# Releasing GpSimd's subtraction by a one-column VectorE copy, and reordering ScalarE's work, in a fused attention and two-layer kernel

## The chip, the cores and the metric

The kernel runs on one core of one Trainium2 chip. The metric is the device time of one execution in microseconds (us). Engines are named as in the profile: PE is TensorE (its weight loads are PEld), DVE is VectorE, ACT is ScalarE, POOL is GpSimd, SP is SyncE, which issues nearly all DMAs in one queue, in order.

## The reference, cut to what matters

Three stages follow one another on 2304 tokens (4 x 576) of 512 features:

```python
# chunked attention: 8 heads of 64, softmax inside chunks of 64 tokens
scores = scale * q_c @ k_c^T;  attn = softmax(scores);  x = attn @ v_c
# first network, w_in 512 x 2048, w_out 2048 x 512
h = x @ w_in;  x = (h - tanh(h)) @ w_out
# second network, same sizes
h = x @ w_in;  y = (h * tanh(softplus(h))) @ w_out
```

All of it is float32. The kernel reaches float32 accuracy by splitting each operand into a high and a low part (type fp32r) and adding three products, hi*hi, hi*lo and lo*hi (THREE, L338).

## The kernel before, in words

**Blocks and steps.** The tokens are cut into five blocks (BLOCKS, L38: 512, 256, 512, 512, 512). For each block the first network's 2048 hidden features are walked in NF = 16 tiles of 128. One (block, tile) pair is a step; there are NS = 80, in the list `steps` (L328), and the loop at L811 goes through them. In step s PE computes the hidden tile (`gemm1`, L340, 12 matmuls into one of two PSUM banks, `hidden(s)`) and, some steps later, multiplies it by w_out into four banks that gather the block's output (`gemm2`, L350, 12 matmuls). From step 36 on gemm2 lags by three steps (`lag`, L503): gemm2(s-3) is issued in step s. In step 38 no gemm2 is issued, because the lag grows there.

**The gap between them.** h - tanh(h) loses digits for small h, so a polynomial is used there. For step s:

- `gap_act` (L394), on ACT: Square of the bank into z, and Tanh into t. Between the two a list `between` is run, in the late steps `hi_part(s-2)`.
- `gap_mid` (L401), on DVE: the product g = z * bank, and the difference t = bank - t. Both read the PSUM bank.
- `gap_poly` (L407), on ACT: Relu of z into the mask m, and a second Square, which writes z in place. It therefore waits until DVE's product has read z.
- `gap_end` (L388), on DVE and one step later: g = (z + PK) * g (L390), and COPY_PREDICATED of t into g by the mask (L391).
- `hi_part` (L412), on ACT: the high part of g into go[:, 0]. `lo_part` (L428), on POOL from step 32 on: the low part, g minus the high part, into go[:, 1] (helper line L82). gemm2 reads both.

**Order inside a late step** (s > `late` = 36; the branch at L835). Each engine takes its instructions in the order in which the loop writes them: gemm1(s); DVE's gap_end(s-1); ACT's Square(s), hi_part(s-2), Tanh(s); POOL's lo_part(s-2), released by ACT's high part; DVE's gap_mid(s); the plan `inner`; `second(s)`, which issues gemm2; the plan `outer`; ACT's gap_poly(s); then the plans `cast` (ACT), `tail`, `w_again` (reloads of weights) and `job` (DVE and SP).

**Attention in between.** Tiles of 128 tokens of the next block are computed in four steps s to s+3 (L482 to L498). Step s: `a_scores` on PE (inner), then in the tail `a_first`, that is `a_max` on DVE and `a_exp` on ACT. Step s+1: `a_norm` on DVE. Step s+2: `a_turn`, transposes on PE, after gemm2, and `a_turned` on ACT, which copies them to SBUF as et (tail). Step s+3: `a_values` on PE, between gemm1 and gemm2, reads et; `a_part` writes the high part (ACT, L323) and the low part (DVE) of the block's x (tail).

**Units.** From step `first_job` = 35 on, the second network's weights are turned on the chip into sums and differences for a fast matrix product (seven products in place of eight) and stored in DRAM as win and wout. The table JOBS (L517) has a row for each of 16 units: its number, the step of its load (1 MB, `j_load`, SP), and the steps of its casts on ACT (j_turn L104, j_low L189, j_hi L210) and its work on DVE (join L113, sums and low parts L82). Five units are loaded at once when the pool "j" opens in step 35 (L816). Odd weights w of the first network are kept in DRAM as w1s and reloaded by `w_again` (L168, DMA at L175) when a slot of the ring of three is free.

**The end of the first network.** From step 69 (XFROM) x chunks are loaded into one tile `spare` (L422) and split (`x_sum`, `x_split`) in steps 73 to 78. In memory the pool "late" takes the place of the pool "j". After the loop come the last parts of the gap, gemm2 of the last steps, and `evacuate(NB-1)` with its stores of x1 (L377). The weights of the second network are loaded by `wf_load` (L594), cast by `wf_hi` (ACT) and `wf_lo` (DVE). `wf_lo` issues the next load (L611 to L617):

```python
elif part and j % 2:
    wf_load(p, j - 1, 1)
elif part and j + 3 < NJ:
    wf_load(p, j + 3, 1)
```

So the load of (0, 0, 1) is issued by wf_lo(0, 1, 1), behind the stores of evacuate in SP's queue. After that the loop at L931 runs `group1` (product1, L631) and `phase2` (slot2, L732) three times.

**Homes of the first weights.** At the start the first four token tiles are loaded whole into the slots of weights that come later: `home((0, NF - 3, NF - 1, NF - 2)[i])` (L234), that is w13, w15 and w14; those three weights are loaded after the first attention (L471). Slots lie in the pool in the order in which they were first taken, so w14's comes first in the pool "w", whose place the pool "f" (wf_load) takes over at the end.

Of the kernel before, what the change touches and what calls it, by code (L numbers as in the profile page):

```python
# [8 lines left out]
F32 = mybir.dt.float32  # L9
# [15 lines left out]
SQ_SCALE = PD ** 0.5  # L25
# [22 lines left out]
def attn_moe_moe(ctx, tc, qkv, w1, w2, out):  # L48
# [182 lines left out]
    def a_load(i, part=None):  # L231

        if 0 < i < first[1]:
            pool, tag = home((0, NF - 3, NF - 1, NF - 2)[i])  # L234
            t = pool.tile([P, 2 * DM], I64, tag=tag, name="qkv", bufs=1)[:].bitcast(F32)[:, :3 * DM]
            QK[i], V[i] = t[:, :2 * DM], t[:, 2 * DM:]
            nc.sync.dma_start(out=t, in_=qkv[i])
            return
        if part != 1:
            QK[i] = pools["a"].tile([P, 2 * DM], F32, tag="qk", name="qk", bufs=1)  # L240
            nc.sync.dma_start(out=QK[i], in_=qkv[i][:, :2 * DM])
        if part != 0:
            V[i] = pools["a"].tile([P, DM], F32, tag="v", name="v", bufs=2)
            nc.sync.dma_start(out=V[i], in_=qkv[i][:, 2 * DM:])
# [82 lines left out]

    steps = [(b, f if b != 3 else NF - 1 - f) for b in range(NB) for f in range(NF)]  # L328
# [65 lines left out]
    def gap_act(s, between=()):  # L394
        ph = hidden(s)
        z, t, m, g = ZT[s] = temp(s, "z"), temp(s, "t"), temp(s, "m", BF16), temp(s, "g")
        nc.scalar.activation(z, ph, AF.Square)  # L397
        run(*between)
        nc.scalar.activation(t, ph, AF.Tanh)  # L399
# [7 lines left out]
    def gap_poly(s):  # L407
        z, t, m, g = ZT[s]
        nc.scalar.activation(m, z, AF.Relu, bias=-C2)
        nc.scalar.activation(z, z, AF.Square, scale=SQ_SCALE, bias=SQ_BIAS)  # L410
# [9 lines left out]
    XG = {}  # L420

    def spare(k, n):  # L422

        if not XG:
            XG[0] = xp.tile([P, KD, 2 * TMAX], F32, tag="x1", name="spare")
        return XG[0][:, k, :n]
# [12 lines left out]
    for f in range(NF - 3):  # L439
        w_load(f)  # L440
# [18 lines left out]
    def run(*todo):  # L459
# [11 lines left out]
        (a_load, lead), (a_load, lead + 1, 1), (w_load, NF - 3), (w_load, NF - 2), (w_load, NF - 1),  # L471
# [4 lines left out]
    first_job = 2 * NF + 3  # L476
    inner, outer, tail, head, mid, post = {}, {}, {}, {}, {}, {}
# [4 lines left out]
    for b in range(1, NB):  # L482
        for q in range(BLOCKS[b] // P):
# [4 lines left out]
            at(tail, s, (a_first, i))  # L488
# [3 lines left out]
            at(outer if s + 2 > first_job + 1 else inner, s + 2, (a_turn, i))  # L492
            at(tail, s + 2, (a_turned, i))
            at(inner, s + 3, (a_values, i))
            at(tail, s + 3, (a_part, i, 0))
# [16 lines left out]
    def units(s, ahead):  # L512
# [7 lines left out]
        (9, 35, 41, 41, 44, 44, 45, 46, 47, 46, 47),  # L520
        (1, 35, 42, 43, 45, 45, 46),
        (10, 35, 43, 44, 46, 48, 48, 49, 50, 49, 51),
# [32 lines left out]
    def x_load(c):  # L555
        p, c = divmod(c, 4)
        t = pools["x"].tile([P, 4, TH // 2], F32, tag=("xa", "xb")[c % 2], name="xs")[:] if p else (
            spare(c, 2 * TH).rearrange("p (q n) -> p q n", q=4))
# [49 lines left out]
    def wf_lo(p, j, part):  # L608
        t = W2[p, j, part]
        sub(t[:, 1], WF.pop((p, j, part)), t[:, 0].bitcast(F32))  # L610
        if part == 0 and j + 2 < NJ:  # L611
            if p + j:
                wf_load(p, j + 2, 0)
        elif part and j % 2:
            wf_load(p, j - 1, 1)
        elif part and j + 3 < NJ:
            wf_load(p, j + 3, 1)  # L617
# [184 lines left out]
    late = first_job + 1  # L802
    XFROM = 4 * NF + 5

# [6 lines left out]
    for s in range(NS):  # L811

        if s == first_job:
            eo.close()
            pools["j"] = er.enter_context(tc.tile_pool(name="j", bufs=1, side="right"))
            for n, start, *_ in JOBS:  # L816
                if start == first_job:
                    j_load(n)
# [16 lines left out]
        if s > late:  # L835
            gap_act(s, [(hi_part, behind)] if behind >= late else [])
            if behind >= late:
                lo_part(behind)
            gap_mid(s)
            run(*inner.pop(s, []))  # L840
            second(s)
# [60 lines left out]
    assert not streamed and not job and not cast and not tail and not inner and not outer and ends + 6 < NS  # L902
# [23 lines left out]
    wf_load(0, 2, 0)  # L926
    evacuate(NB - 1)
# [56 lines left out]
```

## Time and profile before

| | us |
|---|---|
| median of 3 runs | 857.38 (856.44 to 857.4) |
| the profiled execution, its own time | 856.95 |
| its span in the trace | 855.2 |
| PE busy | 816.2 (95%) |
| PEld busy | 730.6 (85%) |
| DVE busy | 662.3 (77%) |
| ACT busy | 503.6 (59%) |
| POOL busy | 75.7 (9%) |

How to read it: the span is what the trace covers, and 1.75 us lie around it. The shares are means over stages that differ: the first network's steps end at about 500 us, and behind them the second network runs. In the rows a line has the start, the duration, the engine, the line of code, the operation, what is written and read, how many instructions were merged, and in brackets how long the engine stood idle before it and which instruction ended that. L82 and L85 are helpers (subtract, add); there the names of the tiles tell which work it is.

### The profile page before, as it was taken

How to read it: one execution, taken by the hardware profiler on the slowest of the kernel's cores; microseconds unless marked ns; L12 is line 12 of the kernel's file. 1: busy time of each engine (PE TensorE's matmuls, PEld its weight loads, DVE VectorE, ACT ScalarE, POOL GpSimd, SP SyncE). 2: the span in 40 equal slices, each digit the busy share in tenths (PEclk: the TensorE clock that was granted, in tenths of full speed). 3: DMA queues.
4: the chain of work that ended last, by engine and by line, in shares of the span. 5: the costliest groups of instructions: out<-in, count | busy, mean ns of one | idle time of the engine just before them, and what ended most of it. 6: DMA issues, size and time to landing. Idle time of an engine off the chain costs nothing.

```text
span 855.2 us, 13350 instructions
## 1 busy us (share of the span) xinstructions
PE 816.2 (95%) x5244; PEld 730.6 (85%) x5244; DVE 662.3 (77%) x916; ACT 503.6 (59%) x783; POOL 75.7 (9%) x64
## 2 busy tenths in 40 slices
PE   7899999999899979989999889999999999999997
PEld 6677778998677768768888679999999999999997
DVE  6999976865688897888887838878688787587653
ACT  3887966665665676575856535554455456345432
POOL 0001100001111222221221200000000000000000
PEclk9899999999999999999999999999999999999999
DMA  9975526626556686866585144398633788433873
GB/s 371 419 256 114 144 50 225 239 80 259 209 179 247 228 280 212 308 228 217 201 286 200 43 135 130 136 340 293 241 105 93 292 295 298 158 113 134 295 260 112
DMA packets 59071, 180.18 MB, mean 211 GB/s; under 512 B 4736, under 2 KB 32896, under 8 KB 46592
## 3 DMA queue, kind: packets, MB, share of 16 engines
q1 hardware_dynamic: 57568, 174.08, 57.3%
q0 software_dynamic: 1440, 5.24, 3.3%
q8 instruction: 41, 0.67, 0.3%
q14 instruction: 22, 0.18, 0.1%
HBM read 134.22 MB, written 39.85 MB: 204 GB/s over the span
## 4 chain that ended last, share of the span: by engine, by line
PE 57%; DVE 24%; DMA 7%; ACT 6%; issue 5%; SPq 1%; POOL 0%; DVEq 0%; ACTq 0%; POOLq 0%
PE banks L732 21%; PE banks L631 20%; PE banks L355 8%; PE banks L346 7%; DVE unit L82 3%; DVE g L390 3%; DVE g L404 3%; DMA w<-w1s 3%; DVE t L82 2%; DMA w<-wf 2%; DVE unit L113 2%; DVE wf L113 1%; DMA wout<-unit 1%; DVE g L391 1%; ACT unit L104 1%
## 5 line engine op out<-in xcount | busy, mean ns | idle before, releaser
L355 PE MATMUL banks<-go,w 128*128 128x512 f32 (+1 forms) x960 | 224.8, 384 | 7.0 <-POOL go L82 3.3
L346 PE MATMUL banks<-x,w 128*128 128x512 f32 (+1 forms) x960 | 218.7, 376 | 8.6 <-DMA w<-w1s 3.1
L355 PEld LDWEIGHTS banks<-go,w 128*128 128x128 f32 x960 | 172.4, 194 | 44.8 <-POOL go L82 4.7
L346 PEld LDWEIGHTS banks<-x,w 128*128 128x128 f32 x960 | 169.0, 191 | 44.5 <-DVE g L404 3.5
L631 PE MATMUL banks<-xo,w 128*128 128x384 f32 x1008 | 176.1, 334 | 3.0 <-ACT w L606 2.6
L732 PE MATMUL banks<-s,w 128*128 128x384 f32 x1008 | 178.6, 340 | 0.0
L631 PEld LDWEIGHTS banks<-xo,w 128*128 128x128 f32 x1008 | 174.7, 188 | 4.0 <-ACT w L606 2.9
L732 PEld LDWEIGHTS banks<-s,w 128*128 128x128 f32 x1008 | 178.1, 188 | 0.0
L82 DVE TENSOR_TENSOR s<-g,s 128x768 fp32r<-128x768 f32 x84 | 79.9, 957 | 44.8 <-ACT s L719 44.4
L719 ACT CAST s<-g 128x768 fp32r<-128x768 f32 x84 | 69.6, 835 | 62.4 <-PE banks L732 57.2
L82 POOL TENSOR_TENSOR go<-g,go 128x512 fp32r<-128x512 f32 x48 | 66.2, 1380 | 311.0 <-ACT go L418 290.9
L410 ACT ACTIVATE z<-z 128x512 f32<-128x512 f32 (+1 forms) x80 | 47.2, 589 | 63.9 <-DVE g L404 62.9
L404 DVE TENSOR_TENSOR g<-z,banks 128x512 f32<-128x512 f32 (+1 forms) x80 | 50.1, 626 | 41.1 <-ACT t L399 41.0
L82 DVE TENSOR_TENSOR w<-wf,w 128x1024 fp32r<-128x1024 f32 (+1 forms) x53 | 58.2, 1099 | 24.1 <-ACT w L606 23.6
L397 ACT ACTIVATE z<-banks 128x512 f32<-128x512 f32 (+1 forms) x80 | 43.9, 549 | 47.9 <-PE banks L346 47.9
L391 DVE COPY_PREDICATED g<-m,t 128x512 f32<-128x512 int16 (+1 forms) x80 | 67.8, 847 | 2.8
L606 ACT CAST w<-wf 128x768 fp32r<-128x768 f32 (+1 forms) x47 | 43.8, 934 | 39.2 <-DMA wf<-win 24.9
L390 DVE SCALAR_TENSOR_TENSOR g<-z,g 128x512 f32<-128x512 f32 (+1 forms) x80 | 58.2, 728 | 3.7 <-ACT z L410 3.7
L643 ACT ACTIVATE g<-g 128x768 f32<-128x768 f32 x36 | 30.5, 847 | 46.5 <-DVE g L85 46.5
L85 DVE TENSOR_TENSOR o<-o,banks 128x768 f32<-128x768 f32 x39 | 37.1, 951 | 19.5 <-PE banks L732 12.6
L82 DVE TENSOR_TENSOR t<-banks,t 128x512 f32<-128x512 f32 (+1 forms) x80 | 50.4, 630 | 0.0
L418 ACT CAST go<-g 128x512 fp32r<-128x512 f32 (+1 forms) x80 | 45.8, 573 | 7.6 <-DVE g L391 7.5
(70 smaller groups left out, 671.6 us busy)
## 6 DMA issues: line engine op xcount, KB each, us to landing
w<-wout SPq DMA_DIRECT2D x42, 1024.0 KB, 5.7
w<-w SPq DMA_DIRECT2D x16, 1024.0 KB, 19.7
unit<-w SPq DMA_DIRECT2D x16, 1024.0 KB, 6.9
w<-w1s SPq DMA_DIRECT2D x15, 1024.0 KB, 6.2
wf<-win SPq DMA_DIRECT2D x23, 512.0 KB, 3.6
wf<-win SPq DMA_DIRECT2D x24, 384.0 KB, 3.1
w1s<-w SPq DMA_DIRECT2D x8, 1024.0 KB, 7.6
qk<-qkv SPq DMA_DIRECT2D x15, 512.0 KB, 5.6
```

What stands on the lines that cost most here:

```text
L82: (eng or nc.vector).tensor_tensor(o, a, b, op=ALU.subtract)
L346: nc.tensor.matmul(ps, w[:, a, k * P:(k + 1) * P], x[:, c, k, :BLOCKS[b]], start=n == 0, stop=n == 3 * KD - 1)
L355: nc.tensor.matmul(banks[:, m, :t], w[:, a, DM + m * P:DM + (m + 1) * P], g[:, c, :t], start=s % NF == 0 and n == 0, stop=s % NF == NF - 1 ...
L390: nc.vector.scalar_tensor_tensor(g, z, PK, g, op0=ALU.add, op1=ALU.mult)
L391: nc.vector.copy_predicated(g, m.bitcast(I16), t)
L397: nc.scalar.activation(z, ph, AF.Square)
L404: nc.vector.tensor_tensor(g, z, ph, op=ALU.mult)
L410: nc.scalar.activation(z, z, AF.Square, scale=SQ_SCALE, bias=SQ_BIAS)
L418: nc.scalar.copy(o[:, 0, :BLOCKS[steps[s][0]]], GF[s])
L631: nc.tensor.matmul(ps, w[:, x, c % 4, k * P:(k + 1) * P], XO[p][:, a, y, k], start=m == 0 and n < 4, stop=m == 5, skip_group_check=n > 3)
L719: nc.scalar.copy(t[:, 0], src)
L732: nc.tensor.matmul(ps[:, m], w[:, x, k % 2 * 2 + e, m * P:(m + 1) * P], s[:, y, e], start=n == 0 and e + jj == 0 and q < 4, stop=n == 2 an ...
```

## The change

- A new function `tick`: a copy on DVE of one column of go's high part over the first column of its low part. It stands between hi_part and lo_part, so POOL's lo_part, which writes over that column, follows DVE's copy. In a late step hi_part(s-2), tick(s-2) and lo_part(s-2) now stand ahead of gap_act(s), and nothing stands between Square and Tanh.
- `gap_poly`'s second Square writes a buffer y of its own: in the pool "j" up to step 69, and from step 70 in the tile `spare`, whose x chunks are packed closer to make room.
- Attention tiles with s > 36: a_exp moves from the tail of step s to the head (`front`) of step s+1, a_turned from the tail of s+2 to the head of s+3, and a_part(i, 0) from the tail of s+3 to a plan `early`, ahead of gap_poly.
- In step 35 two units are loaded instead of five; the other three are loaded at the ends of steps 37, 38 and 39.
- At the start tile 3 goes into the slot of w11 instead of w14, and w11 joins the weights that are loaded late.
- wf_load(0, 0, 1) is issued ahead of evacuate, and wf_lo(0, 1, 1) no longer issues it.

```diff
-            pool, tag = home((0, NF - 3, NF - 1, NF - 2)[i])
+            pool, tag = home((0, NF - 3, NF - 1, NF - 5)[i])
...
-    def gap_act(s, between=()):
+    def gap_act(s):
...
         nc.scalar.activation(z, ph, AF.Square)
-        run(*between)
         nc.scalar.activation(t, ph, AF.Tanh)
...
     def gap_poly(s):
         z, t, m, g = ZT[s]
+        y = z
+        if s > late:
+            y = spare(6 * TMAX + s % 2 * TMAX, TMAX) if s > XFROM else pools["j"].tile([P, TMAX], F32, tag="y", name="y", bufs=2)[:]
+            ZT[s] = y, t, m, g
         nc.scalar.activation(m, z, AF.Relu, bias=-C2)
-        nc.scalar.activation(z, z, AF.Square, scale=SQ_SCALE, bias=SQ_BIAS)
+        nc.scalar.activation(y, z, AF.Square, scale=SQ_SCALE, bias=SQ_BIAS)
+
+    def tick(s):
+
+        nc.vector.tensor_copy(GO[s][:, 1, :1], GO[s][:, 0, :1].bitcast(F32))
...
-    def spare(k, n):
+    late = first_job + 1
+    XFROM = 4 * NF + 5
+
+    def spare(o, n):
 
         if not XG:
-            XG[0] = xp.tile([P, KD, 2 * TMAX], F32, tag="x1", name="spare")
-        return XG[0][:, k, :n]
+            XG[0] = xp.tile([P, 2 * KD * TMAX], F32, tag="x1", name="spare")
+        return XG[0][:, o:o + n]
...
     for f in range(NF - 3):
-        w_load(f)
+        if f != NF - 5:
+            w_load(f)
...
-        (a_load, lead), (a_load, lead + 1, 1), (w_load, NF - 3), (w_load, NF - 2), (w_load, NF - 1),
+        (a_load, lead), (a_load, lead + 1, 1), (w_load, NF - 5), (w_load, NF - 3), (w_load, NF - 2), (w_load, NF - 1),
...
-            at(tail, s, (a_first, i))
+            if s > late:
+                at(tail, s, (a_max, i))
+                at(front, s + 1, (a_exp, i))
+            else:
+                at(tail, s, (a_first, i))
...
-            at(tail, s + 2, (a_turned, i))
+            if s > late:
+                at(front, s + 3, (a_turned, i))
+            else:
+                at(tail, s + 2, (a_turned, i))
             at(inner, s + 3, (a_values, i))
-            at(tail, s + 3, (a_part, i, 0))
+            at(early if s + 3 > late else tail, s + 3, (a_part, i, 0))
...
-        (9, 35, 41, 41, 44, 44, 45, 46, 47, 46, 47),
-        (1, 35, 42, 43, 45, 45, 46),
-        (10, 35, 43, 44, 46, 48, 48, 49, 50, 49, 51),
+        (9, 37, 41, 41, 44, 44, 45, 46, 47, 46, 47),
+        (1, 38, 42, 43, 45, 45, 46),
+        (10, 39, 43, 44, 46, 48, 48, 49, 50, 49, 51),
...
-            spare(c, 2 * TH).rearrange("p (q n) -> p q n", q=4))
+            spare(2 * TH * c, 2 * TH).rearrange("p (q n) -> p q n", q=4))
...
-        elif part and j % 2:
+        elif part and j % 2 and p + j > 1:
             wf_load(p, j - 1, 1)
...
-            for n, start, *_ in JOBS:
-                if start == first_job:
-                    j_load(n)
+            for n in (JOBS[0][0], JOBS[1][0]):
+                j_load(n)
...
         if s > late:
-            gap_act(s, [(hi_part, behind)] if behind >= late else [])
+            run(*front.pop(s, []))
             if behind >= late:
+                hi_part(behind)
+                tick(behind)
                 lo_part(behind)
+            gap_act(s)
             gap_mid(s)
             run(*inner.pop(s, []))
+            run(*early.pop(s, []))
             second(s)
             run(*outer.pop(s, []))
             gap_poly(s)
...
     wf_load(0, 2, 0)
+    wf_load(0, 0, 1)
     evacuate(NB - 1)
```

## Rows read from the trace of the kernel before

**Rows 1.** Busy time of each engine from 206 to 490 us, the late steps:

```profile
core 0: us, PE busy (x) PEld busy (x) DVE busy (x) ACT busy (x) POOL busy (x), PEclk, DMA share, GB/s
206.00:490.00 284.00, 265.32 (x1558) 211.94 (x1557) 235.44 (x332) 188.05 (x309) 60.09 (x44) 0.97 0.63 226
```

**Rows 2.** Waits of PE from 195 to 515 us:

```profile
engine line waited for: us in total, times, longest us
PE banks L311 <- ACT et L299: 10.0, 5, 3.7
PE banks L355 <- POOL go L82: 3.3, 4, 1.0
PE banks L346 <- DMA w<-w1s: 3.1, 1, 3.1
PE banks L631 <- ACT w L606: 2.6, 1, 2.6
PE banks L355 <- ACT go L418: 1.6, 2, 0.8
PE banks L294 <- DVE e L287: 0.7, 1, 0.7
PE banks L631 <- DVE w L82: 0.4, 1, 0.4
```

**Rows 3.** PE in order of time, places from 220 to 507 us:

```profile
220.49 4.33 PE L346 MATMUL banks<-x,w 128*128 128x512 f32 x12 [3.08 <-DMA w<-w1s]
...
286.28 2.91 PE L346 MATMUL banks<-x,w 128*128 128x512 f32 x12
...
381.85 4.59 PE L355 MATMUL banks<-go,w 128*128 128x512 f32 x12
...
455.48 2.91 PE L355 MATMUL banks<-go,w 128*128 128x512 f32 x12
...
506.14 0.62 PE L631 MATMUL banks<-xo,w 128*128 128x384 f32 x2 [2.59 <-ACT w L606]
```

**Rows 4.** Busy time and granted clock behind one long wait (columns as in rows 1):

```profile
381.90:386.30 4.40, 4.40 (x17) 3.47 (x14) 3.57 (x7) 2.38 (x5) 1.46 (x1) 0.61 0.66 204
```

**Rows 5.** ACT in order of time, ahead of that wait:

```profile
377.98 0.63 ACT L410 ACTIVATE z<-z 128x512 f32<-128x512 f32 x1 [1.72 <-DVE g L404]
378.51 1.12 ACT L104 ACTIVATE unit<-unit 128x1024 f32<-128x1024 f32 x1
```

**Rows 6.** DVE in order of time, places from 240 to 483 us:

```profile
240.14 1.86 DVE L391 COPY_PREDICATED g<-m,t 128x512 f32<-128x512 int16 x1
...
296.79 0.68 DVE L404 TENSOR_TENSOR g<-z,banks 128x512 f32<-128x512 f32 x1
...
453.05 0.36 DVE L85 TENSOR_TENSOR xt<-spare 128x192 f32<-128x192 f32 x1 [5.46 <-DMA wout<-unit]
...
455.61 0.67 DVE L404 TENSOR_TENSOR g<-z,banks 128x512 f32<-128x512 f32 x1
...
482.94 1.76 DVE L390 SCALAR_TENSOR_TENSOR g<-z,g 128x512 f32<-128x512 f32 x1
```

**Rows 7.** POOL in order of time, at 240 us:

```profile
240.12 1.29 POOL L82 TENSOR_TENSOR go<-g,go 128x512 fp32r<-128x512 f32 x1 [6.59 <-ACT go L418]
```

**Rows 8.** L391 from 206 to 490 us (durations in ns: minimum/median/maximum):

```profile
L391 DVE COPY_PREDICATED g<-m,t x44: 733/752/1878, 208.1 to 487.5; 128x512 f32<-128x512 int16 x44
```

**Rows 9.** L404, DVE's product, from 206 to 490 us (same columns):

```profile
L404 DVE TENSOR_TENSOR g<-z,banks x44: 660/674/690, 205.8 to 485.4; 128x512 f32<-128x512 f32 x44
```

**Rows 10.** Waits of ACT from 206 to 490 us:

```profile
ACT z L410 <- DVE g L404: 61.0, 42, 4.2
```

**Rows 11.** Waits of DVE from 206 to 490 us:

```profile
DVE x L82 <- ACT x L323: 15.1, 8, 2.7
```

**Rows 12.** DVE's groups, shapes apart, 206 to 490 us (busy us, mean ns, idle before):

```profile
L285 DVE TENSOR_SCALAR rd<-rd 128x8 f32<-128x8 f32 x7 | 1.2, 172 | 0.2
```

**Rows 13.** SP's queue in order of time, two places:

```profile
201.86 2.55 SPq L182 DMA_DIRECT2D unit<-w  x5
...
501.95 8.54 SPq L601 DMA_DIRECT2D wf<-win  x3
```

**Rows 14.** L175, the reloads of w1s (microseconds from issue to landing):

```profile
DMA to landing us min/median/max: 4.6/6.2/15.9
```

More of the change, by code (lines that the diff above doesn't have):

```diff
@@ L325, in a_part @@
             sub(lo, ps, hi.bitcast(F32))
+    first_job = 2 * NF + 3
     steps = [(b, f if b != 3 else NF - 1 - f) for b in range(NB) for f in range(NF)]
@@ L470, in attn_moe_moe @@
         (w_lo, 0), (a_part, 3, 1), (w_turned, 1), (w_float, 1),
-        (a_load, lead), (a_load, lead + 1, 1), (w_load, NF - 3), (w_load, NF - 2), (w_load, NF - 1),
+        (a_load, lead), (a_load, lead + 1, 1), (w_load, NF - 5), (w_load, NF - 3), (w_load, NF - 2), (w_load, NF - 1),
         (w_turned, 2), (w_low, 2))
-    first_job = 2 * NF + 3
-    inner, outer, tail, head, mid, post = {}, {}, {}, {}, {}, {}
+    front, inner, outer, early, tail, head, mid, post = {}, {}, {}, {}, {}, {}, {}, {}
     def at(plan, s, *todo):
@@ L491, in attn_moe_moe @@
             at(head if short(s) else mid if b == 1 else tail, s + 1, (a_norm, i))
-            at(outer if s + 2 > first_job + 1 else inner, s + 2, (a_turn, i))
-            at(tail, s + 2, (a_turned, i))
+            at(outer if s > late else inner, s + 2, (a_turn, i))
+            if s > late:
+                at(front, s + 3, (a_turned, i))
+            else:
+                at(tail, s + 2, (a_turned, i))
             at(inner, s + 3, (a_values, i))
-            at(tail, s + 3, (a_part, i, 0))
+            at(early if s + 3 > late else tail, s + 3, (a_part, i, 0))
             at(post if short(s) else tail, s + 3, (a_part, i, 1))
@@ L800, in phase2 @@
             run(*extra.pop(k, []))
-    late = first_job + 1
-    XFROM = 4 * NF + 5
     def second(s):
@@ L901, in attn_moe_moe @@
             wf_lo(0, 1, 0)
-    assert not streamed and not job and not cast and not tail and not inner and not outer and ends + 6 < NS
+    assert not streamed and not job and not cast and not tail and not inner and not outer and not front and not early and ends + 6 < NS
     nc.scalar.preload_act_table_set("mish")
```

## The prediction, made before the changed kernel ran

> **What bounds the kernel now.** I read the windows first, then PE's waits, PE's order of time around each wait, and last the engine that each wait names. "Step s" is one pass of the loop at L811: gemm1(s), then gemm2 of an earlier step, 24 matmuls of 512 columns on PE. In the stretch of the late steps (from step 37) PE is busy for 265.3 of 284 us, DVE for 235.4, ACT for 188.1 [rows 1]. So PE sets the pace and what can be won is its idle time. It is short, and each piece has a name. From 195 to 515 us PE waited 10.0 us for the turned copy (et), 3.3 + 1.6 us for the two parts of go, 3.1 us for a reloaded weight (w1s), 2.6 + 0.4 us for the first weights of the second network, 0.7 us for a transpose's input [rows 2]. After 515 us PE waits for nothing, so no change there can help.
>
> A long wait is paid twice. The twelve matmuls behind a long et wait take 4.59 us, where the same line takes 2.91 us undisturbed [rows 3]; the clock granted in that stretch is 0.61 of full speed, so most of it runs at 1.2 GHz instead of 2.4 [rows 4]. That is 1.68 us more. The pattern occurs five times: behind three of the five et waits, once behind w1s (4.33 us, so 1.42 more) [rows 3], and once among the last steps, some 1.6 us. Behind the waits of 0.5 to 0.9 us it does not show.
>
> Why is et late? Ahead of that wait ACT's second Square (L410) starts at 377.98 after idling 1.72 us for DVE's product; two casts of about 1.1 us follow, and only then et [rows 5]. DVE's product was late because the COPY_PREDICATED before it was stretched. The first such case shows how: it takes 1.86 us from 240.14 on, while POOL's low part runs from 240.12 to 241.41 [rows 6, 7]; its median is 0.75 us, its longest 1.88 [rows 8]. From there to 482.94 [rows 6] 24 DVE operations with two inputs in SBUF are stretched so, by some 1.06 us each: 25 us of DVE. The product and the difference that follow read a PSUM bank and keep their length beside POOL: the product's 44 stand between 0.660 and 0.690 us [rows 9]. ACT loses 61.0 us in 42 waits for that product, and DVE in turn 15.1 us in 8 waits for ACT's x cast [rows 10, 11]: the two hold each other up.
>
> **The change part by part.** *The one-column copy.* POOL now starts after DVE's tick, and the next two DVE operations are the product and the difference, each 0.67 us, 1.2 us with their overlap. POOL needs 1.3 to 1.4 us [rows 7], so some 0.2 us of it reaches the following operation, and nothing where DVE waits for tanh after the tick. The tick adds no wait of its own: high part, Square and Tanh stand in this order on ACT, and DVE's next instruction waits for Tanh anyhow. Behind the tick queue the product, the attention work and the units; POOL waits for it, and PE's gemm2 for POOL. Its price is not in the trace. Nearest is the 128x8 operation of 0.17 us [rows 12]; a full 512-column product is 0.67 us [rows 9], and nothing at all is the other end. I take 0.2 us, on DVE alone: 43 times make 9 us. Without the 25 us of stretching DVE's work is 210 us in a window that shrinks to some 260, so the spare is 50 us, and even 43 x 0.67 = 29 us would fit.
>
> *Polynomial in its own buffer.* ACT's second Square stops waiting for DVE: the 61.0 us of ACT idling go. What comes late next on ACT is the exp, which waits for DVE's a_max; that sits behind Tanh and has a whole step.
>
> *Order on ACT.* The high part goes ahead of Square, where it waits only for gemm2(s-4), which PE ends before gemm1(s). So Tanh, and the product behind it, come 0.5 us earlier. Exp and turned copy keep their place among ACT's instructions. The x cast moves ahead of the polynomial, so DVE's 15.1 us go and the polynomial comes 0.5 us later, in a step with room.
>
> Together: between transposes and values PE has one gemm1. From the end of the gemm1 before, ACT, no longer held up, needs four operations of some 0.55 us, at most two casts of 1.1 us and et itself, 5 us in all, while PE asks 5.9 us later (gemm2, transposes and gemm1). So the five et waits and their three slow stretches go: 10.0 + 3 x 1.68 = **15.0 us**. The go and transpose waits come from the same backlog: 3.3 + 1.6 + 0.7 + 1.6 of clock = **7.2 us**.
>
> *Unit loads one by one.* Five loads of 1 MB are issued in 2.55 us from 201.86, and the weight load behind them, issued at 204.5, takes 15.9 us to land, against a median of 6.2 [rows 13, 14]. It lands at 220.4; PE wants it at 217.4. With two loads ahead, half the bytes, it lands near 211 to 213. The others follow the next weight load on SP with no wait between, three in a row from about 215, and have four steps until their cast. Gone: 3.08 + 1.42 = **4.5 us**. That stall also let ACT catch up. Without it ACT leaves step 38 (no gemm2, three casts) at 222.7; Square to polynomial of step 39 and one cast end at 226.4, et at 226.9. PE, from 217.4 on, does gemm1, gemm2, transposes and gemm1 and asks at 226.1: **0.8 us** comes back.
>
> *First weights of the second network.* The load that PE waits for is issued at 501.95, after the x1 stores of the last block [rows 13]. It moves ahead of them, and since the first slot of the pool behind it is now w0 instead of w14, it need not wait for step 78's gemm2. It can be there before 500; ACT's cast (0.84 us) and DVE's difference (0.96 us), each behind one operation of 0.8 to 0.95 us, then end by 502.5, and PE wants them at 506.14 - 2.59 = 503.55 [rows 3]. Gone: 2.6 + 0.4 = **3.0 us**. The altered condition at L614 sends w_lo(0,1,1) on to the next branch, a load of (0,4,1) that nobody reads: 0.375 MB, with 3 us of cover or more before the load behind it on SP is wanted.
>
> *The rest at nothing.* At the start w11 is loaded some places later in the same queue; it is first touched in step 7, and a delay by even the four late loads is far less than seven steps. The load of WF(0,0,0) now waits for chunk 1 too, some 4 us later, and has until step 79.
>
> *What the tick makes worse.* In step 73 DVE idles 5.46 us for the unit store whose memory it reuses, and reaches the product of step 74 at 455.61 [rows 6]. The low part of step 72 no longer runs at 451 but behind the tick, from 455.9 to 457.2; PE wants it at 455.7 (gemm2 at 455.48, first matmul on the high part) [rows 3]. Back: 1.5 us, and 0 to 1.6 us of clock, because it lies between the waits without and with it; I take 0.8. Together **2.3 us**. From there DVE's 5.5 us of work per step equal PE's step, and steps 76 to 79 need no further wait.
>
> Sum: 15.0 + 7.2 + 4.5 + 3.0 = 29.7 gone, 0.8 + 2.3 back, so -26.6 us. The profiled execution took 856.95 us (span 855.2 and 1.75 around it), 0.43 below the median of 857.38. On the median: 830.8, rounded to 831.
>
> **The rivals.**
> - *ACT's casts were the cause.* Then half of the et term stays (7.5 us): 838.5. For it: two casts stand directly before et. Against: 1.72 us of idling stand before them [rows 5]. Chance 0.15.
> - *One tile, one wait.* From step 70 the polynomial lies in the tile that the x chunks are loaded into. If waits are kept by tile, ACT waits for those loads, up to 7.8 us: 839. Chance 0.06.
> - *The reloaded weight stays late* because bytes and not order count: 835.5. Chance 0.04.
> - *The lock only moves.* If POOL starts late after the tick, it meets the two-input operation after the difference; the 25 us stay on DVE and only the weight loads gain: 857.4 - 7.5 = 850. Against: the releases by ACT seen now show no such delay. Chance 0.05. The Trainium skill (SBUF — State Buffer, "Who interferes with whom") bears on this: of a DVE operation with two SBUF inputs and a GpSimd operation that reads SBUF the one that starts first keeps the shared ports to its end, and the other stands still. By that rule, with which the stretched rows agree, a POOL started first by the tick wins every such meeting, so the change would be worth 850 and no more if the tick comes wrong.
> - *Slower: DVE's backlog holds POOL.* Low part s-2 must start by 4.2 us after gemm1(s) ends (a step of 5.5, plus 0.23 for the first matmul, less POOL and tick). Now the product of step 49 starts 7.6 us after its gemm1 ended (286.28 + 2.91, to 296.79) [rows 3, 6], and the last steps look alike. If the backlog stays, et waits stay too, and PE stalls 7.6 - 4.2 = 3.4 us more in each of these two runs, with 1.6 us of clock each: +10.0 - 7.5 gives 860. It decides from a backlog of 4.2 us on. Against: the stretching and ACT's idling, which make the backlog, are what is removed; step by step DVE's work (4.6 to 6.2 us) fits the steps and the backlog stays under 3 us until step 73. Chance 0.06.
> - *Nothing to measure*, a mix of these: 0.02.
>
> **The numbers.** My forecast has 0.62. The range reaches from 827, everything gone and nothing back (857.4 - 29.7 = 827.7), to 845, which takes in the first three rivals with a residue; left out are 850 and 860. A measurement of this kernel tells apart about 0.2%, 1.7 us: faster 0.92, same 0.02, slower 0.06.
>
> **What would show it.** COPY_PREDICATED's longest near 0.8 us; POOL released by DVE; ACT's wait for the product gone; no et wait over 1 us but one near step 40; no w1s wait; a new wait of PE for POOL's go of some 1.5 us in step 75; no gap before 507; PE without waits from there as now. I am wrong if PE waits for go in the middle steps, or if et waits of 3 us remain.

## The result, and the profile after

The changed kernel takes 826.27 us (median of 4 runs, 826.05 to 826.38); the kernel before takes 856.91 us (median of 4, 856.04 to 857.4). The ratio is 0.9643 (95%: 0.9627 to 0.966). The profiled executions took 826.30 and 856.95 us: -30.65 us, where -26.6 was predicted. 826.27 lies 0.7 us under the range's lower end of 827. Direction and places are those of the prediction. The size is not, and the experiments show that the parts of the change work together otherwise than it reasoned.

The first part of the page of the changed kernel:

```profile
span 824.5 us, 13385 instructions
PE 803.1 (97%) x5244; PEld 723.8 (88%) x5244; DVE 641.1 (78%) x958; ACT 503.7 (61%) x783; POOL 71.7 (9%) x64
```

The late steps now last from 206 to about 463 us. Their busy times and granted clock, changed kernel (columns as in [rows 1]):

```profile
206.00:463.00 257.00, 254.96 (x1556) 206.34 (x1555) 214.09 (x374) 187.84 (x308) 57.56 (x45) 1.00 0.72 253
```

PE idles 2.0 us of them where it idled 18.7 of 284, the granted clock is 1.00 where it was 0.97, and DVE works 214.1 us where it worked 235.4 [rows 1]: 21.3 us less, although 42 ticks were added. All waits of PE from 195 to 500 us, changed kernel; none of the 15 waits of [rows 2] is left, and these two are new, the first in step 75 and the second in step 40:

```profile
PE banks L356 <- POOL go L82: 1.5, 1, 1.5
PE banks L311 <- ACT et L299: 0.6, 1, 0.6
```

**The ledger.** What each stage won is read from the start times of the same group of matmuls in both kernels. PE in order of time, kernel before: step 40's gemm1 and scores, gemm2 in step 63 and in step 76, the first product of the second network, the first of its second layer.

```profile
228.02 2.99 PE L346 MATMUL banks<-x,w 128*128 128x512 f32 x12
...
231.46 0.65 PE L267 MATMUL banks<-qk 64*64 64x64 f32 x32
...
389.03 2.97 PE L355 MATMUL banks<-go,w 128*128 128x512 f32 x12
...
460.95 2.97 PE L355 MATMUL banks<-go,w 128*128 128x512 f32 x12
...
488.40 4.35 PE L631 MATMUL banks<-xo,w 128*128 128x384 f32 x24
...
498.16 5.39 PE L631 MATMUL banks<-xo,w 128*128 128x384 f32 x30
...
555.95 4.22 PE L732 MATMUL banks<-s,w 128*128 128x384 f32 x23
```

The same places, changed kernel:

```profile
222.93 2.99 PE L347 MATMUL banks<-x,w 128*128 128x512 f32 x12
226.50 0.69 PE L311 MATMUL banks<-et,v 64*64 64x64 f32 x32 [0.58 <-ACT et L299]
227.02 0.65 PE L267 MATMUL banks<-qk 64*64 64x64 f32 x32
...
365.61 2.97 PE L356 MATMUL banks<-go,w 128*128 128x512 f32 x12
...
432.06 0.40 PE L356 MATMUL banks<-go,w 128*128 128x512 f32 x1
433.92 2.79 PE L356 MATMUL banks<-go,w 128*128 128x512 f32 x11 [1.46 <-POOL go L82]
436.55 2.88 PE L347 MATMUL banks<-x,w 128*128 128x512 f32 x12
439.27 1.10 PE L356 MATMUL banks<-go,w 128*128 128x512 f32 x4
...
461.51 4.33 PE L648 MATMUL banks<-xo,w 128*128 128x384 f32 x24
...
471.25 54.27 PE L648 MATMUL banks<-xo,w 128*128 128x384 f32 x312
525.36 4.93 PE L749 MATMUL banks<-s,w 128*128 128x384 f32 x27
```

| stretch, by the changed kernel's start times | change of the lead, us | predicted |
|---|---|---|
| up to gemm1 of step 40 (0.21 of it from the start-up) | -5.09 | w1s -4.5 |
| to the scores of step 40 | +0.65 | +0.8 |
| to gemm2 in step 63 | -18.98 | et waits and slow stretches -15.0, go and transposes -2.84 |
| to gemm2 in step 76 | +1.74 | +2.3 |
| to the second network | -5.21 | last go waits -4.35 |
| to its second layer | -3.70 | first weights -3.0 |
| sum; own times of the executions | -30.59; -30.65 | -26.6 |

Every term came with its sign and in its place, and nearly every gain is larger than its term.

**The mechanism's lines.** DVE's COPY_PREDICATED and the tick, from 206 to 463 us, changed kernel (ns, minimum/median/maximum), and who waits for the tick:

```profile
L392 DVE COPY_PREDICATED g<-m,t x44: 735/747/774, 207.9 to 459.3; 128x512 f32<-128x512 int16 x44
L418 DVE CAST go<-go x42: 126/140/156, 216.1 to 457.2; 128x1 fp32r<-128x1 f32 x42
  POOL go L82: 196.9, 42
```

The longest COPY_PREDICATED was 1878 ns [rows 8] and is 774 ns. Nor is another DVE operation stretched: in the kernel before, 24 of them between 206 and 490 us take over 0.4 us more than the shortest of their shape (1.07 us more on the mean), in the changed kernel from 206 to 463 us none does. The tick, taken at 0.2 us between 0 and 0.67, costs 0.14. The product and the difference that now run beside POOL did not grow (0.69 us each at most; two are shown at step 75 below). The Trainium skill (SBUF — State Buffer, "Who interferes with whom") says that a VectorE instruction with at most one SBUF input, outside the two-port modes, does not contend with GpSimd; these lengths agree.

ACT's two longest waits, same stretch:

```profile
ACT z L398 <- PE banks L347: 52.8, 36, 2.7
ACT e L279 <- DVE e L82: 3.9, 3, 1.7
```

ACT now idles for PE's hidden tile, as the engine that is not the bound should; the 61.0 us for DVE's product [rows 10] and DVE's 15.1 us for the x cast [rows 11] are gone.

SP's queue, changed kernel: the weight's reload behind two unit loads instead of five, the three late ones, and the first weights ahead of the x1 stores (compare [rows 13]).

```profile
201.66 0.81 SPq L182 DMA_DIRECT2D unit<-w  x2
202.51 0.43 SPq L175 DMA_DIRECT2D w<-w1s  x1
...
214.85 1.65 SPq L182 DMA_DIRECT2D unit<-w  x3
...
451.68 1.74 SPq L618 DMA_DIRECT2D wf<-win  x4
469.96 5.20 SPq L378 DMA_DIRECT2D x<-ev  x8
```

The longest landing of such a reload fell from 15.9 us [rows 14] to 8.9, changed kernel:

```profile
DMA to landing us min/median/max: 4.7/6.4/8.9
```

**Step 75**, the new wait. DVE and then POOL in order of time, changed kernel, with "..." between the engines:

```profile
429.82 0.36 DVE L85 TENSOR_TENSOR xt<-spare 128x192 f32<-128x192 f32 x1 [6.16 <-DMA wout<-unit]
...
432.38 0.14 DVE L418 CAST go<-go 128x1 fp32r<-128x1 f32 x1
432.44 0.68 DVE L404 TENSOR_TENSOR g<-z,banks 128x512 f32<-128x512 f32 x1
433.03 0.68 DVE L82 TENSOR_TENSOR t<-banks,t 128x512 f32<-128x512 f32 x1
...
432.60 1.27 POOL L82 TENSOR_TENSOR go<-g,go 128x512 fp32r<-128x512 f32 x1 [11.42 <-DVE go L418]
```

DVE is held up by the unit store, the tick stands behind it, POOL behind the tick, and PE, from 432.46 on, behind POOL: the predicted chain, 1.46 us against 1.5.

### The profile page after: what moved, and what is told of

It reads as the page before. It is cut to its first block, busy times and chain, and to the rows that moved or that the text cites. A ratio compares the mean times of both kernels' runs of the same rounds, so it can differ in the third digit from the quotient of the medians.

```text
span 824.5 us, 13385 instructions
## 1 busy us (share of the span) xinstructions
PE 803.1 (97%) x5244; PEld 723.8 (88%) x5244; DVE 641.1 (78%) x958; ACT 503.7 (61%) x783; POOL 71.7 (9%) x64
## 4 chain that ended last, share of the span: by engine, by line
PE 83%; DVE 8%; DMA 3%; issue 3%; ACT 1%; POOL 0%; SPq 0%; DVEq 0%; POOLq 0%; ACTq 0%
PE banks L749 22%; PE banks L648 21%; PE banks L356 20%; PE banks L347 18%; DMA w<-wf 2%; DMA wout<-unit 1%; DVE wf L113 1%; PE banks L311 1%; PE banks L267 1%; DVE w L109 1%; DMA qkv<-qkv 1%; DVE g L392 1%; PE banks L294 1%; DVE w L82 1%; DVE t L82 1%
## 5 line engine op out<-in xcount | busy, mean ns | idle before, releaser
L356 PE MATMUL banks<-go,w 128*128 128x512 f32 (+1 forms) x960 | 216.2, 374 | 3.6 <-DVE go L82 2.1
L356 PEld LDWEIGHTS banks<-go,w 128*128 128x128 f32 x960 | 166.9, 188 | 37.6 <-DVE go L82 2.9
L648 PE MATMUL banks<-xo,w 128*128 128x384 f32 x1008 | 175.4, 334 | 0.0
L648 PEld LDWEIGHTS banks<-xo,w 128*128 128x128 f32 x1008 | 174.9, 188 | 0.2
L404 DVE TENSOR_TENSOR g<-z,banks 128x512 f32<-128x512 f32 (+1 forms) x80 | 50.4, 630 | 49.2 <-ACT t L399 47.6
L82 POOL TENSOR_TENSOR go<-g,go 128x512 fp32r<-128x512 f32 x48 | 62.2, 1297 | 286.8 <-DVE go L418 196.9
L392 DVE COPY_PREDICATED g<-m,t 128x512 f32<-128x512 int16 (+1 forms) x80 | 55.3, 691 | 2.8
L85 DVE TENSOR_TENSOR g<-o,banks 128x768 f32<-128x768 f32 x36 | 34.3, 953 | 17.2 <-PE banks L648 16.1
L413 ACT ACTIVATE m<-z 128x512 bf16<-128x512 f32 (+1 forms) x80 | 47.3, 591 | 0.0
```

Source lines behind the costliest of these rows:

```text
L82: (eng or nc.vector).tensor_tensor(o, a, b, op=ALU.subtract)
L85: nc.vector.tensor_tensor(o, a, b, op=ALU.add)
L356: nc.tensor.matmul(banks[:, m, :t], w[:, a, DM + m * P:DM + (m + 1) * P], g[:, c, :t], start=s % NF == 0 and n == 0, stop=s % NF == NF - 1 ...
L392: nc.vector.copy_predicated(g, m.bitcast(I16), t)
L404: nc.vector.tensor_tensor(g, z, ph, op=ALU.mult)
L648: nc.tensor.matmul(ps, w[:, x, c % 4, k * P:(k + 1) * P], XO[p][:, a, y, k], start=m == 0 and n < 4, stop=m == 5, skip_group_check=n > 3)
```

## The experiments

Every edit is made to the changed kernel (826.27 us), and "changed" in the tables means that kernel. The first four each undo one part; the next four cross three parts with each other; the last four repeat the changed kernel and try to better it. Kernels 5 to 8 ran on another chip than the other eight, so kernels are compared by the ratio to the kernel before, which ran beside each group, rather than by the time alone. Loss or gain at a place is again a difference of start times between two profiled executions. One repeat shows how far such differences can be trusted: in a second profiled execution of the changed kernel the wait of step 75 is 1.25 us in place of 1.46, and all behind it comes 0.2 us earlier.

**1. Without the tick**, so that POOL is again released by ACT's high part:

```diff
                 hi_part(behind)
-                tick(behind)
                 lo_part(behind)
```

> The changed kernel (826.3 us) without the one-column copy: POOL's low part is released by ACT's high part again, which now stands ahead of Square. Theory A (the stretched DVE operations feed the backlog): POOL starts some 2.7 us earlier in the step, beside gap_end or unit work of the step before, 20 to 40 DVE operations are stretched by 1.06 us again, 20 to 40 us of DVE, and et and go waits come back: 830 to 838 us. The wait in step 75 (1.46 us of idling) goes. Rival B (the loop between ACT and DVE made the backlog, and DVE alone can carry the stretching): within 1.7 us of 826.3, or 1.7 us faster because only the wait in step 75 goes.

Measured: 830.54 us (829.99 to 831.0), ratio to before 0.9677 (0.9658 to 0.9696). The stretching is back. COPY_PREDICATED and the busy times from 206 to 465 us, kernel without the tick:

```profile
L392 DVE COPY_PREDICATED g<-m,t x44: 731/755/1741, 208.0 to 463.5; 128x512 f32<-128x512 int16 x44
...
206.00:465.00 259.00, 255.15 (x1556) 206.16 (x1554) 241.93 (x332) 187.62 (x309) 65.37 (x44) 1.00 0.71 251
```

DVE works 27.8 us more than the changed kernel (214.09 in the same stretch), and in the middle steps PE loses 0.05 us by it. The step 75 wait even goes (-1.74), since POOL no longer stands behind DVE. The loss comes afterwards. PE at the end of the first network, same kernel:

```profile
458.03 2.84 PE L356 MATMUL banks<-go,w 128*128 128x512 f32 x11 [0.54 <-POOL go L82]
460.71 1.55 PE L648 MATMUL banks<-xo,w 128*128 128x384 f32 x8
465.41 4.63 PE L648 MATMUL banks<-xo,w 128*128 128x384 f32 x16 [3.14 <-DVE w L82]
```

DVE reaches the low part of the second network's first weights at 464.14 us (459.95 with the tick). From the interrupted gemm2 to the first L648 PE loses 0.8 us, from there to the next gemm2 5.0. Sum: 0.05 - 1.74 + 0.8 + 5.0 = +4.1, as between the profiled executions (830.43 and 826.30). That the stretching delays PE in the middle steps of this kernel is refuted: with the polynomial in its own buffer and the new order, DVE's slack covers it. The tick earns its 4 us at the end, where no slack is left. The time lies in the range of theory A (830 to 838), but by luck: the et waits that this theory expected did not come.

**2. Polynomial in place again**, the rest as changed:

```diff
-        if s > late:
+        if False:
             y = spare(6 * TMAX + s % 2 * TMAX, TMAX) if s > XFROM else ...
```

> The changed kernel with the second Square of the polynomial written in place again (no buffer y); all else stays. ACT must wait for DVE's product once per late step. Theory A: with the stretching gone the product follows Tanh at once in most steps, so ACT idles only some 0.4 us per step where it idled 1.45 us, and et is late only where DVE is still behind: 826 to 829 us. Rival B (ACT's wait for the product was the main part): most of the 15 us of et waits with their slow clock come back, 832 to 840 us.

Measured: 828.09 us (827.69 to 828.38), 0.9648 (0.963 to 0.9667). ACT again waits for the product, 23.5 us in 34 waits instead of 61.0 in 42. PE's wait at step 40 grows from 0.6 to 1.6 us (+0.98 in start times), the last steps lose another 0.98, step 75 gives back 0.33. ACT's waits for the product from 206 to 465 us, this kernel and then kernel 6 below, which differs from it only in that the tick is left out as well:

```profile
ACT z L414 <- DVE g L404: 23.5, 34, 4.6
...
ACT z L414 <- DVE g L404: 48.3, 37, 4.8
```

Up to 475 us, where the late steps of kernel 6 end, it is 53.4 us in 39 waits there. So somewhat more than half of ACT's idling for the product goes with the stretched operations, and the rest stays with the in-place write.

**3. Five unit loads at once**, as before:

```diff
-        if start > first_job:
+        if start > first_job and n not in (9, 1, 10):
             at(job, start, (j_load, n))
...
-            for n in (JOBS[0][0], JOBS[1][0]):
+            for n in (8, 0, 9, 1, 10):
                 j_load(n)
```

> The changed kernel with five unit loads at once in step 35 again. Both theories expect the w1s wait of 3.1 us with its slow stretch back and the et wait of step 40 (0.58 us) gone. By idle time and clock, as the prediction summed it: 826.3 + 3.1 + 1.4 - 0.6 = 830.2 us. By the shift of PE's start times between the two traces (4.9 us gained before step 40, 0.65 lost there): 826.3 + 4.9 - 0.65 = 830.5 us.

Measured: 831.01 us (830.36 to 831.77), 0.9683 (0.9663 to 0.9702). The weight load behind the five takes 16.2 us to land, and the wait is back. The landings of the reloads, and PE, kernel with five loads:

```profile
DMA to landing us min/median/max: 4.8/6.3/16.2
...
221.44 4.33 PE L347 MATMUL banks<-x,w 128*128 128x512 f32 x12 [3.43 <-DVE rd L285]
```

The row names a small DVE operation, but where PE waits for several things the profile names the one that came last; no other kernel shows PE waiting for L285, and the reload, issued at 205.11, landed at 221.3. In start times +4.92 there and +0.34 just behind; the step 40 wait goes (-0.65), step 75 gives 0.29, and 0.8 is start-up scatter (below): +5.12, as between the profiled executions (831.43 and 826.30). So the loads ahead in the queue are the cause of the late weight, and the 0.65 at step 40 is the price of curing it, as predicted.

**4. First weights loaded late again**:

```diff
-        elif part and j % 2 and p + j > 1:
+        elif part and j % 2:
             wf_load(p, j - 1, 1)
...
     wf_load(0, 2, 0)
-    wf_load(0, 0, 1)
     evacuate(NB - 1)
```

> The changed kernel with the load of (0,0,1) issued by wf_lo(0,1,1) again, behind the x1 stores. By idle time, as the prediction summed it (2.59 + 0.38): 829.3 us. If a wait costs more than the idle time that the trace shows in front of it (the pipeline drains and fills, and matmuls that run alone take 0.5 us instead of 0.23): about 830.0 us, the 3.74 us by which the two kernels differ behind this place.

Measured: 831.98 us (830.21 to 834.45, 5 runs), 0.9689 (0.9668 to 0.971). The wait comes back in nearly its old length, but not at its old price. PE, and then granted clock behind it (columns as in [rows 1]), kernel with late weights:

```profile
472.99 5.39 PE L648 MATMUL banks<-xo,w 128*128 128x384 f32 x30
481.34 52.27 PE L648 MATMUL banks<-xo,w 128*128 128x384 f32 x282 [2.97 <-ACT w L623]
...
481.00:484.00 3.00, 2.66 (x7) 2.17 (x8) 2.57 (x3) 1.24 (x2) 0.00 (x0) 0.50 0.18 37
484.00:487.00 3.00, 3.00 (x11) 3.00 (x11) 2.29 (x3) 2.49 (x3) 0.00 (x0) 0.50 0.46 130
```

The 312 matmuls take 5.39 + 52.27 = 57.66 us, where the changed kernel takes 54.27: 3.39 more, and 2.97 of idle time, 6.36 in all. For some 6 us after the wait TensorE runs at 1.2 GHz. In the kernel before, a wait of 2.59 + 0.38 us in the same place was followed by a granted clock of 1.00 and cost 3.70. The one wait was split by two matmuls, the other was not; whether that decides is not shown. Both expected values are under the median. The runs of this kernel lie up to 4 us apart, and the profiled one is the slowest, with 1.7 us of it from the start-up. The granted clock of the whole execution was 0.990 there and 0.995 to 0.997 in the other four (0.995 to 0.997 in the changed kernel too), and the fastest, 830.21 us, fits the 830.0 that was expected. So the slow stretch may belong to the profiled execution alone; the others left no trace that could show it.

**5 to 8. Which part opens the middle steps?** Experiment 1 left open what the three parts (tick, own buffer y, order on ACT) do without one another. "Order" undone means that the high part stands between Square and Tanh again and that exp, turned copy and x cast are back in the tail; loads and weights stay as changed. The order undone:

```diff
+            gap_act(s, [(hi_part, behind)] if behind >= late else [])
             if behind >= late:
-                hi_part(behind)
                 tick(behind)
                 lo_part(behind)
-            gap_act(s)
...
```

> The changed kernel with ACT's order of before in the late steps: high part between Square and Tanh, exp, turned copy and x cast in the tails. The one-column copy, the buffer y and all loads stay as changed. Theory C (ACT and DVE wait for each other in a loop, and each of the three parts alone opens it): PE's waits for et and go in the middle steps stay away, 826 to 829 us. Rival (the order is what carries the gain): at least half of the 20 us of et and go waits come back, 836 us or more.

> The changed kernel without the one-column copy and with the polynomial in place, so of the three parts only ACT's new order is left (loads as changed). Theory C: the middle steps stay nearly free of waits, and what returns is what the run without the copy showed at the end (4 us): 830 to 834 us. Rival (the stretching by POOL, or ACT's wait for the product, must be gone): et waits of 1 to 4 us come back, 838 to 848 us.

> The changed kernel without the one-column copy and with ACT's order of before; of the three parts only the buffer y is left (loads as changed). Theory C: 828 to 834 us, with 20 or more stretched DVE operations and hardly an et wait, because ACT no longer waits for DVE. Rival (the stretching is the cause): et waits come back, 838 us or more.

> The changed kernel with the polynomial in place and ACT's order of before; of the three parts only the one-column copy is left (loads as changed). Theory C: 828 to 834 us, COPY_PREDICATED never above 0.8 us, ACT's waits for the product shorter than 1 us in most steps. Rival (ACT's wait for the product is the cause whatever POOL does): et waits come back, 838 us or more.

Measured. "Middle" is the loss against the changed kernel in PE's start times from the scores of step 34 to gemm2 in step 63; for the kernel before it is the 18.98 of the ledger, so without w1s and step 40. The last row differs from the others in its loads too, which are the old ones: no run has the new loads and none of the three parts.

| tick | y | order | kernel | us, median | ratio to before (95%) | PE's et waits, us | middle, us |
|---|---|---|---|---|---|---|---|
| yes | yes | yes | changed | 826.27 | 0.9643 (0.9627 to 0.966) | 0.6 in 1 | 0 |
| yes | yes | no | 5 | 826.75 | 0.9635 (0.9621 to 0.965) | 1.0 in 1 | 0.5 |
| no | yes | yes | 1 | 830.54 | 0.9677 (0.9658 to 0.9696) | 0.6 in 1 | 0.05 |
| yes | no | yes | 2 | 828.09 | 0.9648 (0.963 to 0.9667) | 1.6 in 1 | 1.0 |
| no | yes | no | 7 | 833.09 | 0.9702 (0.9685 to 0.9718) | 1.4 in 2 | 2.2 |
| yes | no | no | 8 | 832.75 | 0.9703 (0.9689 to 0.9717) | 3.8 in 3 | 5.4 |
| no | no | yes | 6 | 838.26 | 0.9769 (0.9755 to 0.9784) | 6.5 in 4 | 8.9 |
| no | no | no | before | 856.91 | 1 | 10.0 in 5 | 19.0 |

The parts do not add up. Counted from the kernel before, y alone wins 17 of the 19 us, the tick 14, the order 10; any two of them win 18 or more. One closed loop between ACT and DVE would look like this, and it is argued from the table, not seen in one trace: DVE's stretched work delays the product, ACT waits for the product, and Tanh and the x cast, for which DVE waits, come later. It is nearly enough to cut the loop in one good place, the in-place write. With the order alone ACT still waits 53.4 us for the product in 39 waits (experiment 2), and PE up to 3.6 us for et: that part alone does not do it, and of what was expected the 838 to 848 hold. The tick alone comes out in the time that theory C expected, but not free of et waits (3.8 us in 3), and ACT still waits 33.8 us for the product in 41 waits, though no COPY_PREDICATED takes over 0.8 us.

At the end the tick counts most. The two kernels that have it but lack y lose 1.0 us in the last steps. The three kernels without it lose 5.2 to 6.2 us in the last steps and at the first weights, and get 1.74 back in step 75. Kernels 1 and 7 lose it to the late weight on DVE, kernel 6 to waits for go, as the kernel before did. PE in the last steps of kernel 6 (order only):

```profile
467.67 0.50 PE L356 MATMUL banks<-go,w 128*128 128x512 f32 x1 [0.34 <-ACT go L426]
469.70 4.29 PE L356 MATMUL banks<-go,w 128*128 128x512 f32 x11 [1.53 <-POOL go L82]
```

The granted clock from 469.7 to 474 us was 0.62 there.

**9 to 12. Can the rest be had?** The changed kernel once more; then the tick of step 74 left out, so that in step 75 POOL need not stand behind DVE's delay:

```diff
-                tick(behind)
+                if s != ends + 2:
+                    tick(behind)
```

unit 0's casts a step later, so that ACT has one cast less ahead of et in step 40:

```diff
-        (0, 35, 38, 39, 40, 42, 42),
+        (0, 35, 39, 40, 40, 42, 42),
```

and all of it, with the load that nobody reads left out too:

```diff
-        elif part and j + 3 < NJ:
+        elif part and j % 2 == 0 and j + 3 < NJ:
```

> The changed kernel itself, unaltered, beside the three that follow, so that they are compared on one chip: 826 us.

> The changed kernel without the one-column copy in step 74 alone, where DVE stands idle for the unit store when POOL could start. POOL's low part of step 72 is released by ACT's high part again and runs while DVE idles. If the wait of step 75 costs the 1.46 us of idling that the trace shows: 1.5 us less than the changed kernel; if it costs the 1.74 us by which PE's start times shift there: 1.7 us less.

> The changed kernel with the two casts of unit 0 a step later (steps 39 and 40 instead of 38 and 39). Step 38, which has no gemm2, then has two casts instead of three, and ACT is one cast earlier at the turned copy of step 40. Theory: the et wait of step 40 (0.58 us, 0.65 in start times) goes and nothing comes back, 0.65 us less than the changed kernel. Rival (step 40 now has three casts and delays its own Square): the wait only moves, same time.

> The changed kernel with both edits (no copy in step 74, unit 0 a step later) and without the load of (0,4,1) that nobody reads. If the two waits are independent: 1.74 + 0.65 = 2.4 us less than the changed kernel, with no wait of PE at all between 195 us and the last stores. The unread load is expected to cost nothing; if it does, the gain is more than 2.4 us.

| kernel | us, median of the runs | ratio to before (95%) |
|---|---|---|
| changed again | 826.22 (825.98 to 827.75) | 0.9639 (0.9626 to 0.9653) |
| one tick skipped | 825.68 (825.52 to 826.02) | 0.9631 (0.9617 to 0.9644) |
| unit 0 later | 826.04 (825.69 to 826.71) | 0.9635 (0.9621 to 0.9648) |
| all | 825.09 (824.83 to 825.26) | 0.9622 (0.9609 to 0.9635) |

PE around step 75 and in the last steps, kernel with one tick skipped:

```profile
431.95 2.91 PE L356 MATMUL banks<-go,w 128*128 128x512 f32 x12
434.69 2.88 PE L347 MATMUL banks<-x,w 128*128 128x512 f32 x12
...
458.21 2.84 PE L356 MATMUL banks<-go,w 128*128 128x512 f32 x11 [0.95 <-POOL go L82]
```

Step 75 has no wait left, and gemm1 follows gemm2 by 2.74 us instead of 4.49 (436.55 - 432.06): 1.75 us won by removing a wait that was shown as 1.46. Of this, 1.24 comes back with a wait of 0.95 us at gemm2(77): DVE is late as before, its tick for that step stands at 456.67, and what PE no longer loses in step 75 it asks for earlier here. So the skip is worth 0.5 to 0.6 us where 1.5 or 1.7 were expected, and the 95% intervals of the two ratios overlap. Unit 0 later takes the et wait of step 40 away (-0.65 in start times) and gives 0.3 in step 75; its profiled execution (826.31) lost 1.0 at the start-up, and the median does not tell it apart from the changed kernel. All together is the best of the kernels, 825.09 us: -0.65, -1.74, +1.32 by the start times are -1.07, and the profiled executions (825.26 and 826.30) are 1.04 apart. Of the 2.4 us that were expected, 1.3 come back in the same place: gemm2(77) waits 1.07 us for POOL. For the unread load nothing is left.

## Why the prediction was right in kind and short in size

**The step that failed is the pricing of the terms.** The prediction took each wait at the idle time that the waits view shows ahead of it, added 1.4 to 1.7 us where a slow stretch followed, and set the low end at 827 as "everything gone and nothing back" (29.7 us). Nothing more than those 29.7 us was believed to be there. There were 33.0 (0.2 of it from the start-up), and 2.4 came back instead of 3.1. A wait costs more than its idle time: the work before and behind it also takes longer. In step 75 of the changed kernel the twelve matmuls take 0.40 + 2.79 = 3.19 us instead of 2.91, and 0.28 + 1.46 = 1.74. Waits differ in this. The five et waits of the kernel before, which stand between two groups of matmuls, cost 0.06 to 0.08 us each above their idle time (3.75 became 3.82, the slow stretch apart), so their term was nearly right. Waits for go that stand inside a gemm2, behind its first matmul, cost 0.26 to 0.29 more (0.52 became 0.78 in the kernel before). The idle time and the price of the same places:

| wait of PE | idle shown, us | price by start times, us | granted clock behind |
|---|---|---|---|
| et, step 40, changed | 0.58 | 0.65 | 1.00 |
| go, one tick skipped | 0.95 | 1.24 | 1.00 |
| go, step 75, changed | 1.46 | 1.74 | 1.00 |
| first weights, before (two waits) | 2.97 | 3.70 | 1.00 |
| w1s, before | 3.08 | 4.88 | 0.65 |
| low part of the weights, kernel 1 | 3.14 | 4.99 | 0.63 |
| first weights, kernel 4 | 2.97 | 6.36 | 0.50 |

By the terms: w1s 4.88 against 4.5; the five et waits 10.4 in start times against 10.0; their three slow stretches 4.7 against 5.04; the four go and transpose waits among the middle steps 3.81 against 2.84; the last steps 5.21 against 4.35; the first weights 3.70 against 3.0. The gap to the measured time is 4.0 us. In order: start-up 0.21, w1s 0.38, step 40 0.15, et 0.1, go and transposes 0.97, step 75 0.56, the last steps 0.86, the first weights 0.70, and 0.1 of rounding and of the end. So 2.5 of the 4.0 us lie in the waits for go, for the transposes' input and for the first weights, all priced at their idle time, 0.4 in w1s, and 0.7 in what was to come back (0.56 of it in step 75, where the 0.8 us of clock did not come and the wait itself cost 0.28 more). The range failed for the same reason: its low end was no bound. The time itself is off by 0.5 us more than the gain, because the forecast started from a median of 857.38 for the kernel before, and with the result it is 856.91; 826.27 + 0.47 would still lie under 827.

**Point by point.** *et waits:* right; all five are gone, and the one that was forecast for step 40 came: PE asked at 225.9 us and waited 0.58, where 226.1 and 0.8 were forecast. That the stretched DVE work is what made et late is right for the kernel before (kernel 8: the tick alone removes 14 of 19 us), but not that it has to go for et to be in time: kernel 1 keeps it and has no middle wait. *Tick:* right in price and in queue; that its saving on DVE would pay in the middle steps was not needed, and that it decides the end was not foreseen. *Own buffer:* right, ACT's 61.0 us are gone, and alone it is the strongest part. *Order:* right in sign, worth 0.5 us beside the other two. *Unit loads* and *first weights:* right, shown by undoing the loads of each; the slot of w11 in place of w14's was not undone by itself. *Step 75:* right in place and length; the 0.8 us of clock did not come, the granted clock stayed at 1.00. *At rest, nothing:* nothing is seen of the late w11, and for the unread load nothing is left in the kernel without it.

**The rivals.** *ACT's casts were the cause:* not of the five waits, which are gone while the casts stand as before; of the new one in step 40 they are, since it goes when two casts move a step on (unit 0 later). *One tile, one wait:* no, ACT's polynomial waits for no load of the x chunks. *The weight stays late:* no, 8.9 us at most. *The lock only moves:* no, the longest COPY_PREDICATED is 774 ns, no other DVE operation is stretched, and the tick starts POOL beside the two operations that keep their length. *Slower by DVE's backlog:* its mechanism is real, but shows only where a store holds DVE: 1.74 us in step 75, and 1.24 at gemm2(77) when that is cured.

**What stays open:** why a wait of 2.97 us was followed by the slow clock in kernel 4 and one of 2.59 and 0.38 us in the kernel before was not, and whether it follows in every execution of kernel 4. No run separates it.

## What to carry to other kernels

Price a removed wait by the start times of the work around it, not by the idle time alone, and do not take the sum of all idle times for the best that can come. Where two engines wait for each other in a loop, cut it at the cheapest place, try the parts alone, and expect them not to add up; what a part is worth may lie at the end, where the slack has run out. Releasing GpSimd by a tiny VectorE instruction just ahead of operations that read PSUM cost 0.14 us here and took away stretches of 1 us; beside the other two parts that paid only at the end.

## What the runs showed that was not expected

- A wait of PE costs 0.06 to 0.4 us more than its idle time in this code at full clock, and up to 3.4 us more where 1.2 GHz follows (the table above).
- The clock behind a wait of about 3 us is not settled by its length: 1.00 behind 2.59 and 0.38 us (before), 0.63 behind 3.14 (kernel 1), 0.50 behind 2.97 (kernel 4). Nor need the wait be that long: the first et wait of the kernel before, 1.84 us, was followed by 0.70, the wait of 1.46 us in step 75 by 1.00.
- 27.8 us of extra DVE work, over 259 us, cost PE 0.05 us in the middle steps, and 5.8 us in the last ones and at the first weights.
- The first 190 us differ between executions with the same code there: the scores of step 34 start at 190.95 us (changed), 191.03 (changed again), 191.77 (kernel 3), 191.96 (unit 0 later), 192.67 (kernel 4). Comparisons of half a microsecond between single profiles have to start behind that.
